# New durations in a list schedule, and a first attention head whose low parts are made on two engines

## The chip, the cores and the metric

The kernel runs on one core of one Trainium2 chip. The metric is the device time of one launch in microseconds (us), taken as the median of several runs. A core has five engines that run side by side, each through its own instruction queue, in order: TensorE (PE in the profile; PEld is its weight load), VectorE (DVE), ScalarE (ACT), GpSimd (POOL) and SyncE (SP, which here only issues DMA transfers). They wait for one another by semaphores.

## The reference

Three blocks follow each other. Attention of 2 batches x 8 heads over 768 positions with head size 64 is masked by a hash: a query sees only the keys whose six projection signs equal its own. Its output feeds two gated feed-forward blocks.

```python
q_bits = (np.einsum('bhsd,dk->bhsk', q, proj) > 0)     # 6 bits; k_bits likewise
mask = q_bucket[:, :, :, None] == k_bucket[:, :, None, :]
scores = np.where(mask, scale * q @ k.T, -1e9)
attn = softmax(scores) @ v                             # (1536, 512) over both batches
h = ((x @ w1) * (x @ w2)) @ w3 @ w_out                 # d_ff 1024
y = (sigmoid(h @ w_gate) * (h @ w_val)) @ w_out2       # d_ff 1536
```

The weights come as 64-bit floats and are decoded to 32 bits on the chip.

## The kernel before

**High and low parts.** TensorE multiplies in the 32-bit format fp32r in one pass. To keep the accuracy, an operand is split into a high part (a copy in fp32r) and a low part (the operand less its high part), and three products are added (`three`, L700): high x high, high x low, low x high. High parts are mostly ScalarE's work, low parts VectorE's or GpSimd's.

**Attention.** There are 16 heads of 6 blocks of 128 queries, 96 steps in all. For a step, `emit_qk` (L466) computes the scores of 128 queries by 768 keys in two banks of PSUM (L473, L476); the operands bq, bk, aq and ak hold the low parts, the keys and the hash rows, 64 partitions each, so that the mask is part of the products. `emit_max` (L478) takes the row maximum on VectorE (L482), `emit_exp` (L484) the exponential with the row sum on ScalarE (L492). `emit_T` (L517) transposes the result four tiles at a time on TensorE (L525), ScalarE copies them as high part (L528) and VectorE makes the low part (L530); both are called pt. `emit_av` (L534) multiplies them with v (L543). `emit_x` (L546) adds the two halves into xall with a small PSUM copy on ScalarE (256 elements, L555) and an addition on VectorE (L556).

**Heads.** `prep` (L399) readies a head one head ahead: GpSimd scales q (L409), copies (L410) and subtracts (L411); `hashes` (L388) multiplies with the projections (pq, L393), takes the sign on ScalarE (sg, L395) and compares patterns on TensorE (L396). The first head has nothing to hide behind and has its own code, `first_head` (L429): two loads of each half, ScalarE's high part (L448), VectorE's low part (L449), GpSimd's copies of k into bk and ak (L453), ScalarE's copy of bk's upper half (L454), the hashes, GpSimd's scaling into bq (L456), the thresholds on VectorE (L459) and ScalarE (L461). Its first activation (L437) makes ScalarE load its function table and writes to thr, a tile that holds two thresholds. The constants (L810 to L834) are emitted between its two parts; pq_raw holds the projections, loaded twice on ScalarE's DMA queue (L434, L435), and pq is made from it (L826, L827).

**Filler.** Beside attention, `gen_fill` (L563) decodes w3 and w_out and multiplies them into one matrix wc (wacc, L598), and `gen_first` (L626) runs the first of the three token groups of the first feed-forward block (p and y, through L703) once the first batch's attention is done. `decode` (L331) turns a 128x512 tile of 64-bit floats into 32 bits: two activations (L342, L343), two operations on GpSimd (L344, L345), a shift on VectorE (L346) and an addition (L351).

**The order.** The program is emitted with priorities (`prio`, L845: 100 per attention step). Then `order_engines` (L46) runs a list schedule over all instructions emitted so far: a small simulation in which every instruction has a duration by `cost` (L75), a step between engines (L97), the number of free buffers of each ring, and a DMA estimate (L222 to L225). Whenever an engine is free, it takes the ready instruction with the lowest priority number. The order that results is fixed on every engine, SP's DMA issues among them. It fixes the order alone, no times: on the chip an engine waits for the next instruction in its queue, whatever else is ready.

**The rest.** After the list schedule, `moe` (L718) emits the other token groups of the first block and the whole second block: 52 tiles of 36 matmuls of 512 columns (pa, pb and m, L703), with two, one or no decodes per tile.

Of the kernel before, what the change touches and what calls it, by code (L numbers as in the profile page):

```python
# [10 lines left out]
F32 = mybir.dt.float32  # L11
# [7 lines left out]
ALU = mybir.AluOpType  # L19
# [26 lines left out]
def order_engines(tc):  # L46
# [11 lines left out]
    def count(x):  # L58
        n = 1
        for _, c in list(x.ap)[1:]:  # L60
            n *= c
        return n
# [12 lines left out]
    def cost(k):  # L75
# [3 lines left out]
        banks = [x for x in rd + [i.outs[0]] if (region(x) or ("",))[0] in rings and rings[region(x)[0]][0][0] in ("psT", "psS")]  # L79
        if e == "PE":  # L80
            passes = 1 if "float32r" in str(rd[0].dtype) else 2 if n == 128 else 4
            return n / 2.4 * passes + (16 if passes == 1 else -12 if passes == 2 else 4)
        if e == "Activation":
            return 971 if n == 768 and banks else 50 + n * (0.836 if banks else 1.0)
        if e == "Pool":
            if op == "InstTensorTensor":
                return 40 + n * 2.4 if n < 768 else 2200
            return 100 + n * 1.15
        if e == "DVE":
            if op == "InstCustomDveAnt":  # L90
                return 720
            if op in ("InstTensorTensor", "InstTensorReduce") or (op == "InstTensorScalarPtr" and len(rd) > 1 and count(rd[1]) > 8):
                return 69 + n * (1.04 if banks else 1.4)
            return 585 if op == "InstTensorScalarPtr" and n == 384 else 69 + n * 0.6
# [141 lines left out]
def lsh_attention_moe_moe2_kernel(  # L236
# [47 lines left out]
    def f(ap):  # L284
        return ap.bitcast(F32)
# [12 lines left out]
    nthr = cst.tile([P, 1], F32, name="nthr")  # L298
    zb = cst.tile([P, 1], F32, name="zb")
# [129 lines left out]
    def first_head():  # L429
# [7 lines left out]
        act.activation(out=thr[:, 0:1], in_=zb, func=AF.Exp)  # L437
# [8 lines left out]
        for half in range(2):  # L446
            hs = slice(half * HS, (half + 1) * HS)
            act.activation(out=m["aq"][:, hs], in_=t[0][:, hs], func=AF.Copy, scale=scl[:, 0:1])  # L448
            dve.scalar_tensor_tensor(out=m["bq"][:, hs], in0=t[0][:, hs], scalar=scl[:, 0:1], in1=f(m["aq"][:, hs]),  # L449
                                     op0=ALU.mult, op1=ALU.subtract)  # L450
        load_qk(2)
        for d in ("bk", "ak"):
            pool.tensor_copy(m[d][0:D], t[1][0:D])  # L453
        act_copy(m["bk"][D:P], f(m["bq"][D:P]))  # L454
# [500 lines left out]
```

## Time and profile before

| | |
|---|---|
| median of 3 runs | 811.36 us (809.26 to 812.12) |
| the profiled execution's own time | 809.7 us |
| its span, first to last instruction | 807.5 us |
| granted TensorE clock in the profile | 1.00 of full speed |
| PE busy | 783.1 us (97%), 4016 matmuls |
| PEld busy | 657.3 us (81%) |
| DVE busy | 471.0 us (58%) |
| ACT busy | 512.4 us (63%) |
| POOL busy | 437.0 us (54%) |

A line of a table of groups gives the line of the kernel, the engine, the operation, the tile written and the tiles read, the shapes and the number of instructions; behind the first bar the busy time in us and the mean of one in ns; behind the second bar how long the engine sat idle just before these instructions, and what ended most of that. A timeline gives the start of a stretch of like instructions, how long it is, and how many there are (x2). A wait is named by who waited and who released it. Matmuls overlap, so a busy TensorE need not run at its densest.

### The profile page before, as it was taken

How to read it: one execution, taken by the hardware profiler on the slowest of the kernel's cores; microseconds unless marked ns; L12 is line 12 of the kernel's file. 1: busy time of each engine (PE TensorE's matmuls, PEld its weight loads, DVE VectorE, ACT ScalarE, POOL GpSimd, SP SyncE). 2: the span in 40 equal slices, each digit the busy share in tenths (PEclk: the TensorE clock that was granted, in tenths of full speed). 3: DMA queues.
4: the chain of work that ended last, by engine and by line, in shares of the span. 5: the costliest groups of instructions: out<-in, count | busy, mean ns of one | idle time of the engine just before them, and what ended most of it. 6: DMA issues, size and time to landing. Idle time of an engine off the chain costs nothing.

```text
span 807.5 us, 11531 instructions
## 1 busy us (share of the span) xinstructions
PE 783.1 (97%) x4016; PEld 657.3 (81%) x4016; DVE 471.0 (58%) x721; ACT 512.4 (63%) x946; POOL 437.0 (54%) x460
## 2 busy tenths in 40 slices
PE   5899999999999999999999999999999999999998
PEld 4787788888888888988888888888888888888886
DVE  5999997775989799773553535655422222222222
ACT  5999997785989888783465556767434333343332
POOL 6778885675576565286355556777523233332320
PEclk9999999999999999999999999999999999999999
DMA  8767676544456574130022123343001000010001
GB/s 263 200 180 184 170 209 170 141 110 109 108 148 167 131 178 118 39 113 0 27 79 78 53 79 105 124 137 105 0 1 53 0 1 1 0 53 1 0 1 52
DMA packets 28584, 74.44 MB, mean 92 GB/s; under 512 B 6128, under 2 KB 8432, under 8 KB 28528
## 3 DMA queue, kind: packets, MB, share of 16 engines
q1 hardware_dynamic: 28368, 73.73, 32.5%
q8 instruction: 31, 0.51, 0.3%
q14 instruction: 25, 0.20, 0.1%
q10 hardware_dynamic: 160, 0.00, 0.0%
HBM read 52.83 MB, written 3.19 MB: 69 GB/s over the span
## 4 chain that ended last, share of the span: by engine, by line
PE 82%; DVE 9%; ACT 3%; POOL 2%; issue 2%; DMA 0%; ACTq 0%; SPq 0%; DVEq 0%; POOLq 0%
PE m L703 18%; PE pa L703 18%; PE pb L703 18%; PE av L543 6%; PE tp L525 5%; PE p L703 5%; PE wacc L598 4%; PE y L703 3%; PE s L476 3%; PE s L473 3%; DVE pt L530 2%; DVE sm L482 2%; PE gps L393 1%; DVE w3f L351 1%; DVE da L346 1%
## 5 line engine op out<-in xcount | busy, mean ns | idle before, releaser
L743 DVE TENSOR_TENSOR pb<-pb,a 128x512 f32<-128x512 f32 x52 | 36.3, 699 | 178.0 <-PE pb L703 173.2
L697 POOL TENSOR_TENSOR wal<-xall,wah 128x512 fp32r<-128x512 f32 x36 | 47.6, 1323 | 107.0 <-ACT wah L282 107.0
L525 PE MATMUL tp<-idf,e 128*128 128x128 f32 x576 | 99.0, 274 | 2.8 <-DVE pt L530 1.5
L482 DVE TENSOR_REDUCE sm<-s 128x1 f32<-128x768 f32 x96 | 90.7, 947 | 17.6 <-PE s L476 17.4
L530 DVE TENSOR_TENSOR pt<-tp,pt 128x512 fp32r<-128x512 f32 x144 | 94.6, 680 | 9.5 <-ACT pt L528 8.7
L703 PE MATMUL pa<-x,wah 128*128 128x512 f32 x320 | 99.8, 391 | 0.0
L703 PE MATMUL pb<-x,wbh 128*128 128x512 f32 x320 | 98.6, 389 | 0.0
L492 ACT ACTIVATE e<-s,sm 128x768 f32<-128x768 f32 x96 | 86.8, 907 | 14.6 <-DVE sm L482 14.4
L344 POOL TENSOR_SCALAR dr<-st 128x512 bf16<-128x512 f32 x76 | 73.8, 981 | 40.8 <-issue 20.8
L528 ACT ACTIVATE pt<-tp 128x512 fp32r<-128x512 f32 x144 | 82.7, 601 | 10.7 <-PE tp L525 9.1
L525 PEld LDWEIGHTS tp<-idf,e 128*128 128x128 f32 x576 | 70.6, 140 | 13.9 <-DVE pt L530 4.3
L543 PE MATMUL av<-pt,spv 128*128 128x256 f32 x576 | 78.9, 286 | 2.8 <-DVE pt L530 2.6
L543 PEld LDWEIGHTS av<-pt,spv 128*128 128x128 f32 x576 | 73.0, 190 | 7.6 <-DVE pt L530 5.7
L703 PEld LDWEIGHTS pa<-x,wah 128*128 128x128 f32 x320 | 60.1, 188 | 13.6
L703 PEld LDWEIGHTS pb<-x,wbh 128*128 128x128 f32 x320 | 60.1, 188 | 12.6
L473 PE MATMUL s<-bk,bq 128*128 128x384 f32 x192 | 61.6, 370 | 4.6 <-ACT e L492 4.5
L598 PE MATMUL wacc<-wo,t 128*128 128x512 f32 x192 | 65.7, 414 | 0.2 <-POOL wo L593 0.2
L345 POOL TENSOR_SCALAR da<-da 128x512 f32<-128x512 f32 x76 | 48.8, 647 | 26.1 <-ACT da L342 22.5
L703 PE MATMUL pa<-x,wal 128*128 128x512 f32 x160 | 62.9, 393 | 0.0
L703 PE MATMUL pb<-x,wbl 128*128 128x512 f32 x160 | 62.3, 389 | 0.0
L476 PE MATMUL s<-ak,aq 128*128 128x384 f32 x192 | 60.3, 368 | 0.3 <-ACT aq L461 0.3
L343 ACT ACTIVATE dr<-st 128x512 int16<-128x512 uint32 x76 | 60.1, 790 | 0.0
(146 smaller groups left out, 1822.1 us busy)
## 6 DMA issues: line engine op xcount, KB each, us to landing
st<-in_moe_w_dram SPq DMA_DIRECT2D x32, 512.0 KB, 4.8
st<-in_moe_w_out_dram SPq DMA_DIRECT2D x20, 512.0 KB, 4.2
st<-in_moe_w_gate_dram SPq DMA_DIRECT2D x12, 512.0 KB, 3.3
st<-in_moe_w_val_dram SPq DMA_DIRECT2D x12, 512.0 KB, 3.2
qk<-in_qk_dram SPq DMA_DIRECT2D x15, 384.0 KB, 4.1
rawv<-in_v_dram SPq DMA_DIRECT2D x16, 192.0 KB, 2.5
rr<-row SPq DMA_DIRECT2D x16, 192.0 KB, 4.1
out_dram<-o SPq DMA_DIRECT2D x12, 256.0 KB, 2.0
```

Of the source, the lines that this page charges most:

```text
L343: act.activation(out=r.bitcast(I16)[:, 0::2], in_=lw, func=AF.Copy, scale=2.0 ** -29)
L344: pool.tensor_scalar(out=r.bitcast(BF16)[:, 1::2], in0=f(hw), scalar1=0.0, scalar2=1.0, op0=ALU.mult, op1=ALU.mult)
L473: pe.matmul(s[:, half, :HS], lhsT=m["bq"][:, qs], rhs=m["bk"][:, ks], start=True, stop=False)
L476: pe.matmul(s[:, half, :HS], lhsT=m["aq"][:, qs], rhs=m["ak"][:, ks], start=False, stop=True)
L482: dve.tensor_reduce(out=b, in_=s[:, :, :HS], op=ALU.max, axis=AX.XY, negate=True)
L492: act.activation(out=e.rearrange("p (a c) -> p a c", a=2), in_=s[:, :, :HS], func=AF.Exp, bias=sm, scale=1.0, accum_out=su_t[h][:, t:t + 1],)
L525: pe.transpose(ps[:, i * P:(i + 1) * P], e_t[g - g % 2 + a][:, c * P:(c + 1) * P], idf)
L528: act.activation(out=dh, in_=src, func=AF.Copy)
L530: dve.tensor_tensor(out=d, in0=src, in1=f(dh), op=ALU.subtract)
L543: pe.matmul(acc[:w.shape[1], :2 * P].rearrange("p (a t) -> p a t", a=2), lhsT=w, rhs=r[:, :, c], start=(c == 0 and i == 0), stop=(c == NT ...
L598: pe.matmul(acc, lhsT=t3[x][:, j], rhs=wo[y][:, j], start=(j == 0 and n == 0), stop=(j == NF1 - 1 and n == 2))
L703: mm = pe.matmul(ps, lhsT=lhs[x], rhs=rhs[y], start=start and n == 0, stop=stop and n == 2)
```

## The change

The durations in `cost` are replaced for several kinds of instruction: among them the exponential's 971 ns becomes 890, a small PSUM copy of 256 elements on ScalarE goes from 264 to 415, the six operations of a decode and GpSimd's work get other values, and TensorE's fixed parts change by a few ns. The first activation writes to a tile of its own (warm) and no longer to thr. In `first_head`, half 0 is split as before; of half 1, GpSimd scales q in place, ScalarE copies the high part without a scale, and GpSimd subtracts. ScalarE now copies k into bk's lower half, VectorE copies bk's upper half, and GpSimd copies k into ak. Nothing else is edited; the order of the instructions is computed anew from the new durations.

```diff
--- before.py
+++ after.py
@@ -77,21 +77,30 @@
         rd = [x for x in i.ins if hasattr(x, "ap")]
         n = max([count(i.outs[0])] + [count(x) for x in rd[:1]])
         banks = [x for x in rd + [i.outs[0]] if (region(x) or ("",))[0] in rings and rings[region(x)[0]][0][0] in ("psT", "psS")]
+        es = mybir.dt.size(i.outs[0].dtype)
         if e == "PE":
             passes = 1 if "float32r" in str(rd[0].dtype) else 2 if n == 128 else 4
-            return n / 2.4 * passes + (16 if passes == 1 else -12 if passes == 2 else 4)
+            return n / 2.4 * passes + (18 if passes == 1 else -20 if passes == 2 else 4)
         if e == "Activation":
-            return 971 if n == 768 and banks else 50 + n * (0.836 if banks else 1.0)
+            if banks:
+                return 890 if n == 768 else 490 if n == 512 else 300 + n * 0.45
+            return 70 + n + (100 if es == 2 else 0)
         if e == "Pool":
             if op == "InstTensorTensor":
-                return 40 + n * 2.4 if n < 768 else 2200
-            return 100 + n * 1.15
+                return 100 + n * 2.45 if n < 768 else 2250
+            if op == "InstTensorCopy":
+                return 640 if n == 384 else 100 + n * 0.9
+            return 340 if n < 64 else 110 + n * 1.15 + (190 if es == 2 else 0)
         if e == "DVE":
             if op == "InstCustomDveAnt":
-                return 720
-            if op in ("InstTensorTensor", "InstTensorReduce") or (op == "InstTensorScalarPtr" and len(rd) > 1 and count(rd[1]) > 8):
-                return 69 + n * (1.04 if banks else 1.4)
-            return 585 if op == "InstTensorScalarPtr" and n == 384 else 69 + n * 0.6
+                return 860
+            if op == "InstTensorReduce":
+                return 69 + n * 1.06
+            if op == "InstTensorTensor" or (op == "InstTensorScalarPtr" and len(rd) > 1 and count(rd[1]) > 8):
+                return 150 + n * 0.9 if banks else 100 + n * 1.45
+            if op == "InstTensorScalarPtr" and n == 512 and "int32" in str(i.outs[0].dtype):
+                return 560
+            return 595 if op == "InstTensorScalarPtr" and n == 384 else max(125, 69 + n * 0.6)
         return 600
 
     step = {("Activation", "DVE"): 145, ("Activation", "PE"): 200, ("Activation", "Pool"): 170, ("DVE", "Activation"): 132,
@@ -296,6 +305,7 @@
     thr = cst.tile([P, 2], F32, name="thr")
     scl = cst.tile([P, 1], F32, name="scl")
     nthr = cst.tile([P, 1], F32, name="nthr")
+    warm = cst.tile([P, 1], F32, name="warm")
     zb = cst.tile([P, 1], F32, name="zb")
     pat = cst.tile([P, P], F32R, name="pat")
 
@@ -434,7 +444,7 @@
         act.dma_start(out=pq_raw[0:D], in_=proj)
         act.dma_start(out=pq_raw[D:P], in_=proj)
         dve.memset(zb, -2.0 ** -64)
-        act.activation(out=thr[:, 0:1], in_=zb, func=AF.Exp)
+        act.activation(out=warm, in_=zb, func=AF.Exp)
         for half in range(2):
             hs = slice(half * HS, (half + 1) * HS)
             sync.dma_start(out=t[0][:, hs], in_=qk[0][:, hs])
@@ -443,15 +453,17 @@
         load_qk(1)
         load_v(0)
         yield
-        for half in range(2):
-            hs = slice(half * HS, (half + 1) * HS)
-            act.activation(out=m["aq"][:, hs], in_=t[0][:, hs], func=AF.Copy, scale=scl[:, 0:1])
-            dve.scalar_tensor_tensor(out=m["bq"][:, hs], in0=t[0][:, hs], scalar=scl[:, 0:1], in1=f(m["aq"][:, hs]),
-                                     op0=ALU.mult, op1=ALU.subtract)
+        h0, h1 = slice(0, HS), slice(HS, S)
+        pool.tensor_scalar(out=t[0][0:D, h1], in0=t[0][0:D, h1], scalar1=0.0, scalar2=SCALE, op0=ALU.add, op1=ALU.mult)
+        act.activation(out=m["aq"][:, h0], in_=t[0][:, h0], func=AF.Copy, scale=scl[:, 0:1])
+        dve.scalar_tensor_tensor(out=m["bq"][:, h0], in0=t[0][:, h0], scalar=scl[:, 0:1], in1=f(m["aq"][:, h0]),
+                                 op0=ALU.mult, op1=ALU.subtract)
+        act_copy(m["aq"][:, h1], t[0][:, h1])
+        pool.tensor_tensor(out=m["bq"][:, h1], in0=t[0][:, h1], in1=f(m["aq"][:, h1]), op=ALU.subtract)
         load_qk(2)
-        for d in ("bk", "ak"):
-            pool.tensor_copy(m[d][0:D], t[1][0:D])
-        act_copy(m["bk"][D:P], f(m["bq"][D:P]))
+        act_copy(m["bk"][0:D], t[1][0:D])
+        dve.tensor_copy(m["bk"][D:P], f(m["bq"][D:P]))
+        pool.tensor_copy(m["ak"][0:D], t[1][0:D])
         pss = [hashes(m, half) for half in range(2)]
         pool.tensor_scalar(out=m["bq"][D:P], in0=t[1][D:P], scalar1=0.0, scalar2=SCALE, op0=ALU.add, op1=ALU.mult)
         for half in range(2):
```

## Rows read from the trace of the kernel before

**Rows 1.** Busy us (instructions) of PE, PEld, DVE, ACT, POOL by stretch; clock, DMA share, GB/s

```profile
20.00:100.00 80.00, 74.15 (x482) 63.83 (x483) 77.12 (x119) 75.42 (x151) 64.63 (x77) 1.00 0.72 186
100.00:200.00 100.00, 96.54 (x581) 83.88 (x580) 76.57 (x113) 77.90 (x151) 66.35 (x80) 1.00 0.56 147
200.00:300.00 100.00, 97.06 (x623) 86.35 (x622) 88.80 (x136) 88.92 (x177) 62.35 (x78) 1.00 0.59 147
...
345.00:800.00 455.00, 454.98 (x1986) 371.89 (x1985) 178.77 (x265) 222.38 (x376) 213.35 (x185) 1.00 0.13 45
```

**Rows 2.** TensorE's waits in 20 to 345 us: total us, times, longest

```profile
PE s L473 <- ACT e L492: 3.4, 6, 1.4
PE av L543 <- DVE pt L530: 2.6, 5, 0.8
PE gps L393 <- DVE pt L530: 1.8, 2, 1.3
PE tp L525 <- DVE pt L530: 1.5, 3, 0.7
```

**Rows 3.** Timeline of the start: start us, us, engine, line, operation

```profile
3.51 0.06 DVE L828 MEMSET thr<- 64x1 f32 x1 [2.20 <-ACT thr L437]
...
4.10 1.12 ACT L448 ACTIVATE aq<-qk,scl 128x384 fp32r<-128x384 f32 x2 [0.65 <-DVE scl L834]
...
5.47 0.17 DVE L826 CAST pq<-pq_raw 64x6 fp32r<-64x6 f32 x1
...
5.79 0.98 PE L393 MATMUL gps<-aq,pq 128*128 128x384 f32 x2 [5.79 <-DVE pq L826]
5.82 0.82 POOL L453 CAST bk<-qk 64x768 fp32r<-64x768 f32 x1 [3.85 <-DMA qk<-in_qk_dram]
5.87 2.27 DVE L449 SCALAR_TENSOR_TENSOR bq<-qk,scl,aq 128x384 fp32r<-128x384 f32 x2
6.59 1.15 POOL L453 CAST ak<-qk 64x768 fp32r<-64x768 f32 x1
...
7.59 0.52 PE L393 MATMUL gps<-aq,pq 128*128 128x384 f32 x1
8.18 0.84 ACT L282 ACTIVATE bk<-bq 64x768 fp32r<-64x768 f32 x1 [2.95 <-DVE bq L449]
...
9.04 1.05 ACT L395 ACTIVATE sg<-gps,zb 128x384 fp32r<-128x384 f32 x2
9.11 0.84 POOL L456 TENSOR_SCALAR bq<-qk 64x768 fp32r<-64x768 f32 x1 [1.37 <-ACT bk L282]
...
11.11 1.16 ACT L461 ACTIVATE aq<-gps,nthr 64x384 fp32r<-64x384 f32 x2 [1.02 <-DVE ak L459]
```

**Rows 4.** Line view of L435, the second load into pq_raw

```profile
L435 ACTq DMA_DIRECT2D pq_raw<-in_proj_dram x1: 611/611/611, 1.3 to 1.3; - x1
...
DMA to landing us min/median/max: 4.1/4.1/4.1
```

**Rows 5.** Groups by line and form in 20 to 100 us, of ACT, DVE, POOL

```profile
L492 ACT ACTIVATE e<-s,sm 128x768 f32<-128x768 f32 x26 | 23.5, 905 | 2.6 <-DVE sm L482 2.5
L343 ACT ACTIVATE dr<-st 128x512 int16<-128x512 uint32 x12 | 9.6, 796 | 0.0
...
L282 ACT ACTIVATE xall<-av 64x256 f32<-64x256 f32 x13 | 5.0, 381 | 0.3
...
L351 DVE CUSTOM_DVE_ANT_0 wor<-da,dr 128x1024 uint16<-128x1024 uint16 x8 | 6.3, 790 | 0.0
...
L411 POOL TENSOR_TENSOR bq<-qk,aq 128x384 fp32r<-128x384 f32 x10 | 10.1, 1014 | 0.8
L344 POOL TENSOR_SCALAR dr<-st 128x512 bf16<-128x512 f32 x11 | 9.4, 853 | 0.6
```

**Rows 6.** Timeline of TensorE near 41 us

```profile
40.70 0.27 PE L525 MATMUL tp<-idf,e 128*128 128x128 f32 x1
...
40.99 0.71 PE L525 MATMUL tp<-idf,e 128*128 128x128 f32 x5
```

## The prediction, made before the change was run

> **What bounds the kernel now.** I read the busy table by stretches first, because the change can only act where its instructions run. From 345 us on TensorE is busy 454.98 of 455 us [rows 1]: the two MoE stages are fed without a gap, they are emitted after the list schedule, and no edit touches them. What can move lies ahead of that. In 20 to 100 us TensorE is busy 74.15 of 80 us while VectorE and ScalarE are busy 77.12 and 75.42: there the two elementwise engines are the limit. In 100 to 200 and 200 to 300 us TensorE is busy 96.54 and 97.06 of 100, with VectorE at 77 and 89: TensorE bounds, and loses time only where its queue comes to a matmul whose operand is late. Idle TensorE time in these three stretches is 5.85 + 3.46 + 2.94 = 12.25 us. This is what a better order can win in gaps that show; a busy TensorE can also run below its densest spacing, so it is no strict bound.
>
> Then I asked what ended those gaps [rows 2]. VectorE's low part of the transposed probabilities (pt, L530) ended 2.6 + 1.8 + 1.5 = 5.9 us of them, the exponential (e, L492) 3.4 us. So the gaps come from elementwise results that the order puts later than TensorE's queue assumes. Last I read the first 12 us as a timeline [rows 3], for the first head.
>
> **Part 1, the warm-up activation gets its own tile.** Before, the Exp that loads the table wrote thr, so VectorE's memset of thr waited for it 2.20 us, with all the constants, scl and the pq copies queued behind [rows 3]. That wait goes. What is late next is the second small load into pq_raw: issued at 1.3 us and landing 4.1 us later, at 5.4 [rows 4]. Its copy at 5.47 is what the first matmul at 5.79 needs (pq is one tile), and in the planner's arithmetic the pq copies are due before the first low part, so in VectorE's queue that low part still stands behind them, at 5.87 [rows 3]. The 2.20 us are therefore worth 0 here; if that load landed early, they would be worth up to 2.20 us at the first low part, which I do not expect, as the issue is not touched.
>
> **Part 2, low parts on two engines.** Before, both low parts of bq are VectorE's: two of 2.27 / 2 = 1.14 us, so they end at about 7.0 and 8.14 [rows 3]. ScalarE's copy of bk's upper half stands ahead of the Sign in its queue, waits for the second low part, and runs 8.18 to 9.02. So the Sign starts only at 9.04, although the hash matmuls of half 0 end at 7.59 + 0.52 = 8.11 [rows 3]. After: the copy that waits for bq is VectorE's, and ScalarE copies the half of bk that needs only the loaded k (there at 5.82, since GpSimd starts on it then; 0.84 us, so it ends near 6.7). Sign of half 0 can then start at about 8.11 + 0.2 = 8.3, 0.74 us sooner. The 0.2 is my allowance for the step from TensorE to ScalarE; VectorE's end at 8.14 to ScalarE's start at 8.18 bounds such a step below, by 0.04.
>
> Half 1: GpSimd now scales 64x384 (half of the elements of the bk cast that took 0.82 us, so some 0.4 to 0.6), ScalarE makes aq (both halves were loaded by 4.66, the start of its second at the latest), and GpSimd makes the low part. The planner has the ak copy due before aq of half 1, so GpSimd does the copy first: 5.82 + 0.82, or 1.15 when it is disturbed, then one subtraction of 128x384 at 1014 ns [rows 5]: it ends between 7.7 and 8.0. That leaves half 1 no later than the 8.14 of before. Sign of half 1 follows half 0's, each half of the 1.05 us pair, and ends at 9.4 to 9.75 instead of 10.09. Behind it the chain is the same code, up to the ReLU at 11.11 [rows 3]. GpSimd's scaling of bq at 9.11 now waits for VectorE's copy, which no row of 64x768 prices; between 0.35 (nothing but the shorter half of ScalarE's 0.84) and 1.15 (the slowest of the same shape) I take 0.84, the same shape on ScalarE. It starts at 8.0 and ends at 8.9, so 9.11 holds. **I take 0.7 us gained**, between 0 and 1.5. It persists, because the stage behind it is bound by VectorE and ScalarE, which then start sooner.
>
> What speaks against this part is a row: each VectorE low part took 1.14 us while GpSimd's two casts ran beside it, and GpSimd's second cast of the same shape took 1.15 us beside it against 0.82 for the first [rows 3]. The first low part ends 0.4 us after the first cast does. So the two engines seem to take turns, and "at the same time" may not be had. [...] Taking turns in full, cast 0.82, low part 0.4, subtraction 1.01 from 5.82 give 8.05 for half 1, still not after 8.14; hence the 0.7 stands, and comes from ScalarE's queue more than from the second engine.
>
> **Part 3, new durations in the planner.** The instructions of the rest stay; their order on each engine, the SP queue's DMA issues among them, is computed anew. A decode cost the planner 562 + 562 (ScalarE), 689 + 689 (GpSimd) and 376 + 720 (VectorE) = 3598 ns and now costs 582 + 682, 889 + 699 and 560 + 860 = 4272 (the new 560 for int32 also applies to uint32, as it is asked for by name). The trace has means of 796 for the int16 one, 853 for the bf16 one, 790 for the addition into wor [rows 5]. The small PSUM copy goes from 264 to 415, the trace's mean being 381. In 20 to 100 us there are about 12 decodes: VectorE is now planned 12 x 324 = 3.9 us longer in 80 us, GpSimd 12 x 210 = 2.5, ScalarE 12 x 140 = 1.7 plus 13 copies x 0.151 = 2.0 and less 26 exponentials x 0.081 = 2.1 (971 to 890). So in the old plan VectorE had some 5% of room that the chip did not have [rows 1], and the planner pulled fill work of later steps into it, ahead of the low parts for which TensorE then waited. With the room gone, less is pulled ahead.
>
> The price: between all of the 12.25 us of gaps won and as much lost (nothing in the trace excludes a worse order). The gaps that this error makes are the 5.9 us behind pt. Half of these is my value, **3.0 us**, nearer to the small end, because the exponential's 3.4 us, TensorE's own order and the loads are not what was repriced. What is late next is the exponential behind the row maximum, on the same two engines.
>
> **Sum.** 0 + 0.7 + 3.0 = 3.7 us. The profiled execution took 809.7 us, with a span of 807.5; it would become 806.0 and 803.8. The median of the three runs is 811.36, 1.7 above the profiled one, and loses the same: **807.7 us**. About 0.3%, 2.4 us, is what a measurement of this kernel can tell from no change.
>
> **Rivals.**
> - *The new order only moves gaps* (0.27): the first head gives its 0.7 or nothing, and waits won in one stretch return in another, since 20 to 100 us has no room on VectorE in any order. 810.7 us. For it: the stage after 345 us needs the same work whatever the order. Against it: gaps of 2.94 to 5.85 us in stretches with the same kinds of work say that order matters.
> - *Slower, by transposes priced too short* (0.20). Five transposes in a row took 0.71 us with a last one of 0.27, so 0.11 us each [rows 6]. The planner had 94.7 ns and now has 86.7: its TensorE is now further ahead of the chip's, while VectorE and ScalarE are priced right. It would plan the attention products right behind low parts that are in truth ready, or late, by other amounts, and place its fill matmuls where no gap is. The added error is 8 ns x 576 transposes = 4.6 us; if each of it became waiting, with the first head's 0.7, the time is 811.4 + 4.6 - 0.7 = 815.3. It decides if TensorE's waits for pt grow in 100 to 300 us, where it bounds. Against it: TensorE waits in order, so a transpose that takes longer than planned also gives pt more time.
> - *The first head gains nothing* because the two engines take turns longer than above or ScalarE's queue places bk's copy between the two Signs (half 1 then at about 10.1 as before): 808.4 with the reorder's gain, 811.4 without. A chance of 0.08 stands for it beside the reorder's gain; beside no gain it is part of the first rival.
> - *A larger gain*: all gaps behind pt go and the first head's 0.7: 811.4 - 5.9 - 0.7 = 804.8; it is part of the forecast's chance.
>
> **Numbers.** Forecast with the larger gain: 0.45, of which 0.03 falls within 0.3%. First head nothing: 0.08, faster. Only moved: 0.27, all within. Slower: 0.20, of which 0.18 goes beyond 0.3%, the rest within. That gives faster 0.50, same 0.32, slower 0.18. The range runs from 802.0 (the 5.9 us behind pt, half of the exponential's 3.4 and 1.5 at the start: 811.4 - 5.9 - 1.7 - 1.5 = 802.3) to 815.0 (just short of the slow rival in full). The forecast's own range is 803 to 809.5.
>
> **What would show it.** Right: Sign of the first head at 8.3 instead of 9.04, no wait of VectorE for thr, the first matmul still near 5.8; TensorE's idle time in 20 to 300 us near 9 us, with the waits for pt halved; TensorE full from 345 us or a little before, and the MoE stages as long as now. Wrong: a first matmul much before 5.5 (then the pq load was not the gate); Sign at 9.0 or later; idle time in 100 to 300 us above 8 us with more waits for pt (the slow rival); or a TensorE full from the same 345 us although the gaps moved.

## The result and the profile after

Six runs of the changed kernel have a median of 820.06 us (819.39 to 824.5), six of the kernel before, on the same chip, 811.0. The ratio is 1.0121, interval [1.0107, 1.0135]: slower by 1.2%, where a gain of 0.5% was forecast; it lies outside the range. The profiled execution took 819.47 us, with a span of 817.6 against 807.5 us. So 10.1 us are to be explained.

The busy table by stretches, to be held against [rows 1]: stretch, its length, then busy us (instructions) of PE, PEld, DVE, ACT, POOL, the granted clock, the DMA share, GB/s.

```profile
20.00:100.00 80.00, 70.18 (x450) 61.52 (x448) 74.74 (x112) 69.75 (x138) 54.46 (x68) 0.96 0.66 176
100.00:200.00 100.00, 95.18 (x582) 83.79 (x583) 79.67 (x117) 82.23 (x160) 67.77 (x82) 1.00 0.55 144
200.00:300.00 100.00, 97.29 (x622) 86.96 (x621) 85.03 (x131) 85.50 (x170) 62.45 (x74) 1.00 0.56 142
345.00:800.00 455.00, 452.35 (x1978) 368.13 (x1977) 184.02 (x270) 225.10 (x381) 215.58 (x189) 1.00 0.14 47
```

In 20 to 100 us TensorE does 450 matmuls where it did 482, VectorE and ScalarE are less busy too, and the granted clock is below 1.00 for the first time. In 200 to 300 us nothing is lost. From 345 us on, 2.65 us are idle where 0.02 was. TensorE's waits in 20 to 345 us (total us, times, longest), to be held against [rows 2]:

```profile
PE s L485 <- ACT e L504: 7.1, 5, 2.6
PE wacc L610 <- ACT wo L291: 1.9, 1, 1.9
PE tp L537 <- DVE ft L428: 1.3, 2, 0.7
PE wacc L610 <- ACT t L291: 1.2, 1, 1.2
PE av L555 <- DVE ft L428: 1.0, 1, 1.0
PE av L555 <- DVE pt L542: 0.9, 2, 0.5
PE wacc L610 <- POOL wo L605: 0.9, 1, 0.9
...
PE gps L403 <- DVE pt L542: 0.3, 1, 0.3
PE tp L537 <- DVE pt L542: 0.2, 1, 0.2
```

The waits for pt fell from 5.9 to 1.4 us. What took their place are waits for the exponential, 7.1 where it was 3.4, for decoded weights (wo, t), 4.0 where it was 0.2, and for the hash rows of a coming head (ft), 2.3 where it was 0.5.

The start of the changed kernel as a timeline (start us, us, engine, line, operation, and in brackets the idle time before and who ended it), to be held against [rows 3]:

```profile
5.40 0.17 DVE L838 CAST pq<-pq_raw 64x6 fp32r<-64x6 f32 x1 [1.64 <-DMA pq_raw<-in_proj_dram]
...
5.66 0.82 POOL L466 CAST ak<-qk 64x768 fp32r<-64x768 f32 x1 [1.29 <-DMA qk<-in_qk_dram]
...
5.72 0.66 PE L403 MATMUL gps<-aq,pq 128*128 128x384 f32 x1 [5.72 <-DVE pq L838]
5.80 2.05 DVE L459 SCALAR_TENSOR_TENSOR bq<-qk,scl,aq 128x384 fp32r<-128x384 f32 x1
6.45 0.99 POOL L462 TENSOR_TENSOR bq<-qk,aq 128x384 fp32r<-128x384 f32 x1
...
8.96 0.58 ACT L405 ACTIVATE sg<-gps,zb 128x384 fp32r<-128x384 f32 x1 [2.48 <-PE gps L403]
...
11.63 0.58 ACT L405 ACTIVATE sg<-gps,zb 128x384 fp32r<-128x384 f32 x1
...
15.73 0.90 ACT L504 ACTIVATE e<-s,sm 128x768 f32<-128x768 f32 x1
```

VectorE's wait for thr is gone and its pq copy waits for the load instead, so the first matmul stays at 5.72. The low part of half 0 now takes 2.05 us where each took 1.14, and ends at 7.85, 0.41 us after GpSimd's subtraction does (6.45 + 0.99 = 7.44). The second Sign starts at 11.63, and the first exponential at 15.73; before it was at 14.1.

**Where the 10.1 us arise.** I took the same instruction (the k-th exponential, attention product, or product of the later stage) in both traces and subtracted the starts. The change is behind by 1.6 us at the first exponential, by 8.6 at the product that stood at 146.2 us before, by 5.2 at 353 us, by 8.6 at 421.6 us and by 10.1 at 795. So: 1.6 us at the start, 7.0 lost between there and some 150 us (most of it by 105), 3.4 won back up to 353 us, 3.4 lost between 353 and 421 us, 1.5 after that. Their sum is 10.1. This sets one execution against one other; two executions of the same order can differ by some us at such a point, as a pair of runs below shows.

### The profile page after: what moved, and what is told of

It is laid out like the page before. It is cut to its first block, busy times and chain, and to the rows that moved or that the text cites. A ratio compares the mean times of both kernels' runs of the same rounds, so it can differ in the third digit from the quotient of the medians.

```text
span 817.6 us, 11540 instructions
## 1 busy us (share of the span) xinstructions
PE 783.8 (96%) x4016; PEld 660.1 (81%) x4016; DVE 476.7 (58%) x721; ACT 515.0 (63%) x946; POOL 435.1 (53%) x461
## 4 chain that ended last, share of the span: by engine, by line
PE 82%; DVE 8%; ACT 4%; issue 2%; DMA 2%; POOL 1%; SPq 0%; ACTq 0%; DVEq 0%; POOLq 0%
PE m L715 18%; PE pb L715 17%; PE pa L715 17%; PE av L555 6%; PE tp L537 5%; PE p L715 5%; PE wacc L610 3%; PE s L485 3%; PE s L488 3%; PE y L715 2%; DVE pt L542 2%; PE gps L403 2%; DVE sm L494 1%; DMA rr<-row 1%; ACT pt L540 1%
```

## The experiments

What was weighed: that the new durations give a worse order (by transposes priced too short, or otherwise); that the first head's new code costs, at the start or by what it does later; and that any new plan moves the time by some us either way. An expectation calls them theories A, B and C. It also names earlier runs by short labels, which stand in brackets where these runs are told. Medians and ratios are against the kernel before, on the same chip, with 95% intervals. "Behind by" is always the difference of starts against the kernel before, as above. Where medians of two runs are subtracted, they can come from different chips; the kernel before had medians of 810.7 to 811.9 us on them, so such a difference is good to about 1 us. In the cuts of code, `...` stands for lines left out.

**The parts.** Only `cost` changed, with the old head and no warm tile (e1):

> The new durations on the first head of before. Theory A (the new durations give a worse order): most of the 9 us loss is here, 816 to 819 us, with TensorE idle some 4 us more in 20 to 100 us and a gap of 2 to 3 us near 365 us at the start of the MoE part. Theory B (the first head's later start, 1.6 us, and the order that follows from it): 811 us or less, within 2 us of before. Theory C (any new order lands a few us away, up or down): between 805 and 819, not the same losses in the same places as in the changed kernel.

812.25 us, ratio 1.0019 [1.0004, 1.0035]. Only the head and the warm tile changed, with the old durations:

> The new first head with the durations of before. Theory A: 812 to 813 us, the 1.6 us of the later first exponential and no more, the gaps after 20 us as in before. Theory B: 816 to 820. Theory C: the start is 1 to 2 us late and the rest lands anywhere between 806 and 818. In all of them the second half's subtraction on GpSimd and the first half's on VectorE take turns: the VectorE one ends after 7.4 us as in the changed kernel, if GpSimd's order is the same.

819.25 us, 1.0102 [1.0085, 1.0118]. Of these two the head is the one that loses, although its code ends before 15 us: in this run the first exponential is 0.8 us early, and the kernel is still 7.2 us behind from 127 us on. (The turns that the expectation names did not happen here: VectorE's low part began at 5.12 us, ahead of GpSimd's copy at 5.43, and took 0.62 us.) The new durations alone are 2.7 us ahead at 353 us in their trace (a gain of the size forecast) and 2.0 behind at 421 us. Where the head-only kernel loses, near 60 us, as a timeline:

```profile
60.29 2.70 POOL L518 TENSOR_TENSOR xall<-xall,rr 128x768 f32<-128x768 f32 x1 [3.23 <-DMA rr<-row]
...
62.94 0.50 POOL L411 CAST aq<-qk 128x384 fp32r<-128x384 f32 x1
...
63.49 0.69 PE L394 MATMUL gps<-aq,pq 128*128 128x384 f32 x1 [2.60 <-POOL aq L411]
```

and its busy table from 63.1 us on (columns as in the table of stretches above; the number behind POOL's is the clock):

```profile
63.10:69.90 6.80, 6.33 (x20) 5.64 (x21) 1.64 (x3) 3.08 (x7) 5.00 (x7) 0.50 0.55 125
```

GpSimd normalises two finished heads (xall by rr, `emit_scale`) and waits 3.23 us for the load of rr, which landed 9.3 us after its issue (6.3 in the kernel before, which has no wait there). Behind it in GpSimd's queue stands the readying of a coming head (aq), and TensorE's queue has come to that head's hash product. TensorE stalls 2.60 us, and then has a granted clock of 0.50, the half clock below, for 6.8 us. That is most of the loss: 0.6 us behind at 58.6, 5.8 at 77.7.

**Is it any new plan?** One step time of the planner, 10 ns more, in the old kernel:

```diff
-("PE", "Activation"): 197
+("PE", "Activation"): 207
```

> The kernel of before with one planner figure changed by 10 ns (the step from TensorE to ScalarE, 197 to 207), which says nothing truer or falser of the chip. Theory A: 810 to 812 us, as before. Theory C: the order changes in many places and the time moves by 2 us or more, either way (805 to 817).

812.77 us, 1.0015 [1.0, 1.003]. Only TensorE's new fixed parts (the transposes' price among them):

```diff
-return n / 2.4 * passes + (16 if passes == 1 else -12 if passes == 2 else 4)
+return n / 2.4 * passes + (18 if passes == 1 else -20 if passes == 2 else 4)
```

> Only TensorE's new durations (transposes 8 ns shorter, one-pass matmuls 2 ns longer), all else as before. The prediction's slow rival (transposes priced too short, TensorE's waits for pt grow in 100 to 300 us) expects up to 815 us. Theory A without that rival: 810 to 812. Theory C: a move of 2 us or more either way.

812.69 us, 1.0023 [1.0009, 1.0037]. These two new plans cost 0.2% each, not 1.2%. The transposes' price costs no more than that, alone or with all the other new durations (the first run, 1.0019). The slow rival as I had priced it is out.

**The warm tile, and its address.** Old kernel with the warm tile alone:

```diff
+warm = cst.tile([P, 1], F32, name="warm")
...
-act.activation(out=thr[:, 0:1], in_=zb, func=AF.Exp)
+act.activation(out=warm, in_=zb, func=AF.Exp)
```

> The kernel of before with the tile warm alone (no other edit of the first head, old durations). The tile takes 32 bytes of each partition and moves all tiles behind it, xall and wc among them, by 32 bytes. Address theory, from the runs of the changed kernel and of the new head alone, where the matmuls of 430 to 600 us stood 2 to 5 ns further apart than before: the same spacing here (100 us of 500 to 600 hold 432 matmuls instead of 436), 1.5 to 2 us lost behind 400 us, 812.5 to 813.5 us. Rival (the slower spacing comes from the order of the decodes' work, not from addresses): spacing as before, 811 to 812 us. The wait of VectorE for thr is gone in both, and the first matmul is not earlier than the second load into pq_raw.

813.26 us, 1.0024 [1.0008, 1.004]. It is 0.5 us ahead at 380 us and 1.3 behind at 611, with the instructions of that stretch in the same order: it loses 1.8 us where nothing waits. The tile stands among the constants and so, as I reckon, moves all tiles allocated behind them; no run prints addresses, so neither that nor by how much is shown. So I let the Exp write to a third column of thr, with no tile more, first in the head-only kernel:

```diff
-thr = cst.tile([P, 2], F32, name="thr")
+thr = cst.tile([P, 3], F32, name="thr")
...
-warm = cst.tile([P, 1], F32, name="warm")
...
-act.activation(out=warm, in_=zb, func=AF.Exp)
+act.activation(out=thr[:, 2:3], in_=zb, func=AF.Exp)
```

> The new first head with the old durations, the Exp writing to a third column of thr, so that no address moves. Address theory: the 1.7 us behind 400 us come back, and the loss ahead of 100 us stays (the normalisation of the first heads on GpSimd waiting for its row load near 60 us, TensorE idle behind it and then at half clock): 817 to 818 us. Rival: 819 as with the tile.

816.72 us, 1.0053 [1.0031, 1.0074], from nine executions between 812.5 and 818.7 and one of 1103.68, which the ratio leaves out. Its first exponential is 1.5 us late where that of the head-only kernel was 0.8 early, with the same order on VectorE, GpSimd and the DMA issues. When the loads land decides: VectorE's second copy from pq_raw ran at 5.61 us instead of 4.72, so the low part of half 0 began at 6.01, behind GpSimd's copy (5.86), and took 2.04 us instead of 0.62. The same edit in the changed kernel:

> The changed kernel with the Exp writing to a third column of thr, so that all addresses are those of before. By the runs so far the spacing of 500 to 600 us returns to 435 or 436 matmuls, and 1.5 to 1.8 us come back: 818 to 818.7 us.

818.53 us, 1.0096 [1.0076, 1.0117]. The busy rows of 500 to 600 us, first of the warm tile alone, then of the changed kernel with the third column:

```profile
500.00:600.00 100.00, 100.00 (x430) 80.50 (x429) 50.90 (x80) 60.09 (x101) 61.67 (x61) 1.00 0.24 78
```

```profile
500.00:600.00 100.00, 100.00 (x436) 81.51 (x435) 53.64 (x85) 62.84 (x106) 65.43 (x65) 1.00 0.27 89
```

TensorE is busy without a gap in both and starts 430 or 436 matmuls (435 in the kernel before). Each of the six profiled kernels with the extra tile falls back by 1.6 us between 421 and 611 us, and each of the thirteen without it by 0.0. That the tile costs this is shown: 1.5 us of the 10.1 in the changed kernel. That it does so by the addresses it moves is my inference, since the instructions of that stretch and their order are the same; no run shows an address, or why one would matter there.

**The first head's pieces.** Only the low part of half 1 (and its scaling) to GpSimd, in the old kernel:

```diff
...
+pool.tensor_scalar(out=t[0][0:D, h1], in0=t[0][0:D, h1], scalar1=0.0, scalar2=SCALE, op0=ALU.add, op1=ALU.mult)
...
+act_copy(m["aq"][:, h1], t[0][:, h1])
+pool.tensor_tensor(out=m["bq"][:, h1], in0=t[0][:, h1], in1=f(m["aq"][:, h1]), op=ALU.subtract)
```

> Old durations, old copies of k into bk and ak, old thr; only the low part of half 1 goes to GpSimd, with its scaling. If the split is the harmful part: GpSimd's three operations and VectorE's low part take turns, the first Sign is at 9 us or later, and the kernel is 815 to 820. If it is not: 810 to 813.

818.75 us, 1.008 [1.0052, 1.0108]. Its start as a timeline:

```profile
5.53 0.82 POOL L455 CAST bk<-qk 64x768 fp32r<-64x768 f32 x1 [1.16 <-DMA qk<-in_qk_dram]
5.59 1.75 DVE L828 CAST pq<-pq_raw 64x6 fp32r<-64x6 f32 x1
6.32 0.99 POOL L452 TENSOR_TENSOR bq<-qk,aq 128x384 fp32r<-128x384 f32 x1
...
7.48 0.66 PE L393 MATMUL gps<-aq,pq 128*128 128x384 f32 x1 [7.48 <-DVE pq L828]
```

VectorE's copy of 64x6 elements, 0.17 us before, takes 1.75: it starts with GpSimd's cast and ends with GpSimd's subtraction. VectorE did not get in between the two GpSimd instructions. In the kernel before, where GpSimd had two copies instead of a copy and a subtraction, it did: there the first low part ended at about 7.0 us, during GpSimd's second copy, which took 1.15 us instead of 0.82 (6.59 to 7.74). The first matmul comes 1.7 us later, the first exponential 3.4, and the half clock follows in 30.0 to 33.4 us.

Only the copies moved, in the old kernel (e8), and the same with the Exp in the third column:

```diff
-for d in ("bk", "ak"):
-    pool.tensor_copy(m[d][0:D], t[1][0:D])
-act_copy(m["bk"][D:P], f(m["bq"][D:P]))
+act_copy(m["bk"][0:D], t[1][0:D])
+dve.tensor_copy(m["bk"][D:P], f(m["bq"][D:P]))
+pool.tensor_copy(m["ak"][0:D], t[1][0:D])
```

> Old durations, both low parts on VectorE as before, old thr; only the copies move (bk lower half to ScalarE, bk upper half to VectorE). By the prediction's account of ScalarE's queue this gives the Sign at about 8.3 instead of 9.04 us and 0.7 us at the start: 810 to 811 us if the order behind it stays good. If any shift of the first head by a microsecond changes which load the normalisation near 60 us waits for, it may be 814 to 819 as well.

> Old durations, moved copies, third column of thr. The first exponential 1 us or so sooner than before (13.1 to 13.6). If nothing behind it stalls: 809.5 to 810.5 us, faster than both kernels; by e8 (812.0, the same without the third column) rather 811 to 813.

812.02 us, 1.001 [0.9992, 1.0028], and 811.79 us, 1.0007 [0.999, 1.0024]. The first exponential is 0.9 and 1.5 us early, the third 1.1 and 0.4 late. So a gain at the first head is real and is gone two steps later. Where it goes, the third step shows, as a timeline of this kernel (third column) and then of the kernel before:

```profile
13.63 0.69 PE L473 MATMUL s<-bk,bq 128*128 128x384 f32 x1 [1.11 <-ACT e L492]
...
14.97 0.84 PE L393 MATMUL gps<-aq,pq 128*128 128x384 f32 x2
...
17.95 0.96 DVE L482 TENSOR_REDUCE sm<-s 128x1 f32<-128x768 f32 x1 [4.43 <-PE s L476]
```

```profile
15.14 0.45 PE L473 MATMUL s<-bk,bq 128*128 128x384 f32 x1 [1.18 <-ACT e L492]
...
15.88 0.51 PE L393 MATMUL gps<-aq,pq 128*128 128x384 f32 x2
...
17.59 0.96 DVE L482 TENSOR_REDUCE sm<-s 128x1 f32<-128x768 f32 x1 [2.64 <-PE s L476]
```

From the step's first score product to its row maximum the same products, in the same order on TensorE, take 17.95 - 13.63 = 4.32 us here and 17.59 - 15.14 = 2.45 before: 1.9 us more, as much as the gain that is lost between the first and the third exponential. TensorE is the limit there: it is busy without a gap (5.80 of 5.80 us in 13.8 to 19.6). A pair of matmuls of 384 columns takes 0.84 us here, as at a granted clock of 0.50 (the head-only kernel has such a pair at 66.02 us, in its half-clock stretch), and 0.51 before. The first stretch with the full clock, 1.00, begins in the trace's clock records at 19.65 us here and at 13.75 in the kernel before; in 10 to 13.7 us TensorE was busy 2.49 us here and 3.43 there. It is not this trace alone: in the thirteen traces with an edited first head the full clock begins at 15.5 to 23.2 us, in those with the old one at 13.0 to 13.8 (five) or at 18.2 and 18.6 (two). Why it begins later, no run shows.

The changed kernel with both low parts on VectorE again (e9):

```diff
...
-pool.tensor_tensor(out=m["bq"][:, h1], in0=t[0][:, h1], in1=f(m["aq"][:, h1]), op=ALU.subtract)
+for half in range(2):
+    hs = slice(half * HS, (half + 1) * HS)
+    act.activation(out=m["aq"][:, hs], in_=t[0][:, hs], func=AF.Copy, scale=scl[:, 0:1])
+    dve.scalar_tensor_tensor(out=m["bq"][:, hs], in0=t[0][:, hs], scalar=scl[:, 0:1], in1=f(m["aq"][:, hs]),
+                             op0=ALU.mult, op1=ALU.subtract)
```

> The changed kernel with one part undone: both low parts of the first head are VectorE's again; new durations, the moved copies and the warm tile stay. If the split is what costs (the run with it alone gave 818.75, the run with the copies alone 812.0): 811 to 815 us, with the 1.7 us of the moved addresses in it, and the first exponential at 13 to 14 us. If the loss belongs to the whole of the new order: 818 to 821.

817.43 us, 1.0081 [1.0061, 1.0101]: the first exponential is 1.5 us early, and the kernel 8.3 behind at 97.3 us. Then the changed kernel with one edit that keeps GpSimd free beside VectorE's low part:

```diff
-pool.tensor_copy(m["ak"][0:D], t[1][0:D])
+act_copy(m["ak"][0:D], t[1][0:D])
```

> The changed kernel with the copy of k into ak on ScalarE instead of GpSimd, so that GpSimd has nothing between its scaling and its low part. Turn-taking theory: GpSimd's subtraction runs from about 5 to 6 us, VectorE's low part ends by 6.6 us instead of 7.85, the first Sign stands near 8 us instead of 8.96 and the first exponential 1 us or more sooner than 15.73; the whole kernel 1 to 4 us below 820, if the order behind stays alike. Rival (VectorE's low part is slow by itself, or for its operand): it ends at 7.5 or later again.

816.13 us, 1.0075 [1.0051, 1.01]. Its start as a timeline:

```profile
5.04 0.99 POOL L462 TENSOR_TENSOR bq<-qk,aq 128x384 fp32r<-128x384 f32 x1 [0.64 <-ACT aq L291]
...
6.29 0.62 DVE L459 SCALAR_TENSOR_TENSOR bq<-qk,scl,aq 128x384 fp32r<-128x384 f32 x1
...
8.01 0.58 ACT L405 ACTIVATE sg<-gps,zb 128x384 fp32r<-128x384 f32 x1 [0.86 <-PE gps L403]
...
13.39 0.90 ACT L504 ACTIVATE e<-s,sm 128x768 f32<-128x768 f32 x1 [1.01 <-DVE sm L494]
```

With GpSimd idle beside it the low part takes 0.62 us instead of 2.05, and the Sign starts at 8.01. So the turns are shown, and the first exponential comes 15.73 - 13.39 = 2.3 us sooner without them. The whole gains 3.9 us by it (820.06 - 816.13), and 5 us are still lost, with the head now early: they are lost behind it.

**The wait behind the load of rr.** The planner lets an instruction be held behind another. I held GpSimd's normalisation of a pair of heads behind the readying of the first head of the pair after the next, first in the head-only kernel (e11) and then in the kernel before:

```diff
...
+for p in range(NH // 2 - 2):
+    Tiles.holds.append((late["scale", p].name, late["bq", 2 * p + 4].name))
 order_engines(tc)
```

> The new first head with the old durations (819.25 us), and the planner held back so that GpSimd's normalisation of a pair of heads stands behind the readying of the head two further on, not ahead of it. If the loss near 60 us is GpSimd's queue (it waited 3.2 us for the row load, and TensorE 2.6 us for the readying behind it, and then ran at half clock): no such wait, no half clock near 63 us, 812 to 815 us. If the loss comes with the later loads whatever stands in GpSimd's queue: 817 to 820.

817.93 us, 1.0092 [1.0072, 1.0113]. The wait near 60 us and the half clock are gone (0.8 us behind at 77.7, where the head-only kernel had 5.8), but it is 4.5 behind at 97.3, 3.0 at 237.6 and 5.8 at 299.1. So this wait was where that trace lost its time, but the order that comes without the wait loses nearly as much elsewhere.

> The kernel of before with the hold alone. If the hold only changes the place of an operation that nobody is waiting for: 810 to 812. If it costs by itself (the 3 us that e11 lost behind 230 us): 813 to 815.

812.7 us, 1.0009 [1.0, 1.0019]. In the old order, where the load was in time, the hold is worth nothing.

**Put together.** New durations, old head, third column:

> New durations, first head of before, and the Exp in a third column of thr (no wait of VectorE for it, no moved address). If the planner's new figures are worth what the trace of e1 showed ahead of 345 us (2.5 us) and lose it again at the handover to the MoE part (VectorE and GpSimd taking turns there, a half clock of 3.4 us): 810 to 813 us. If the start a little sooner lets another stall happen ahead of 105 us: 814 to 818.

813.01 us, 1.0000 [0.9989, 1.0011]. In its trace it is 4.9 us behind at 105 us and 1.5 behind at 353, although VectorE, ScalarE, GpSimd and the DMA issues have the very order of the first run, which was 2.7 ahead there. So one order can come out 4 us apart in two executions, and the 2.7 us are not a gain to count on. New durations, moved copies, third column, the hold, and both low parts on VectorE (e14):

> New durations, moved copies, both low parts on VectorE, third column of thr, and GpSimd's normalisation held behind the readying of the head two further on. If the stall near 67 us of e9 (TensorE waiting 2.6 us for that readying) is the normalisation ahead of it: the stall is gone and the kernel is 809 to 813. If not: 815 to 817 as e9 without its 1.7 us of addresses.

805.71 us, 0.9914 [0.9897, 0.993]: faster than both. The same without the hold, and the same with the low parts split (which is the changed kernel with the third column and the hold):

> e14 without the hold. If the hold is what let the new durations keep their gain: TensorE stalls again between 60 and 105 us behind GpSimd's readying, and the kernel is 812 to 817 us (e9, the same with moved addresses, was 817.4, of which 1.7 are addresses: 815.7). If the hold did little and e14 was fast for its copies and durations: 805 to 808.

> e14 with the second low part on GpSimd, that is, the changed kernel with the hold and the third column. If the split costs by the start it delays (first exponential 1.5 us later than before against 0.7 earlier in e14) and by what follows from it: 808 to 814, 2 to 8 us over e14. If the split costs nothing once the stall is gone: 805 to 807.

817.01 us, 1.0064 [1.0044, 1.0083], and 810.57 us, 0.9981 [0.9969, 0.9992]. So with the new durations the hold is worth 817.01 - 805.71 = 11.3 us, and the split costs 810.57 - 805.71 = 4.9. The timeline of the kernel without the hold, where it loses:

```profile
63.61 2.23 POOL L524 TENSOR_TENSOR xall<-xall,rr 128x768 f32<-128x768 f32 x1 [3.13 <-DMA rr<-row]
...
66.84 0.45 PE L402 MATMUL gps<-bq,pq 128*128 128x384 f32 x1 [2.42 <-POOL bq L420]
...
100.59 0.44 PE L482 MATMUL s<-bk,bq 128*128 128x384 f32 x1 [2.91 <-ACT e L501]
...
101.47 2.50 POOL L524 TENSOR_TENSOR xall<-xall,rr 128x768 f32<-128x768 f32 x1 [2.29 <-DMA rr<-row]
```

and its busy table behind these two stalls (the clock is the number behind POOL's):

```profile
67.80:71.20 3.40, 3.40 (x16) 3.30 (x14) 1.68 (x4) 2.34 (x5) 3.16 (x5) 0.51 0.85 173
101.90:105.30 3.40, 3.40 (x14) 2.95 (x14) 2.13 (x3) 2.82 (x7) 3.40 (x3) 0.50 0.14 54
```

The first stall is the chain of the head-only kernel again: the load of rr late, GpSimd standing, the coming head's bq behind it, a stall of TensorE, the half clock. The second is another: TensorE waits 2.91 us for an exponential, and the late load of rr comes only behind that. With the hold the order on GpSimd is the other way round (timeline of the kernel with the hold):

```profile
62.94 1.02 POOL L420 TENSOR_TENSOR bq<-qk,aq 128x384 fp32r<-128x384 f32 x1
64.68 2.26 POOL L524 TENSOR_TENSOR xall<-xall,rr 128x768 f32<-128x768 f32 x1 [0.72 <-DVE sm L491]
...
101.08 1.02 POOL L420 TENSOR_TENSOR bq<-qk,aq 128x384 fp32r<-128x384 f32 x1
102.06 2.22 POOL L524 TENSOR_TENSOR xall<-xall,rr 128x768 f32<-128x768 f32 x1
```

Neither normalisation waits for its load, and neither half-clock stretch is there (one of 3.4 us at 24.5 is left). At 353 us this kernel is 4.1 us ahead of the one before, and the kernel without the hold 2.7 behind. The two have the same order up to the first of these normalisations and differ on every engine behind it, so the 11.3 us are what the whole new order is worth: of the 9.8 us by which the traces part between 58.6 and 421.6 us, 4.5 arise by 77.7, with the first stall.

Lined up so that each kernel differs from the one ahead of it by one edit, the runs give the change in steps (third column of thr up to the last step): new durations 1.0000, with the moved copies 1.0064, with the low parts split 1.0096, with the tile warm 1.0121, each known to about 0.2%. The moved copies alone are 1.0007. So half of the loss comes from two edits that cost nothing one by one, and the hold turns just that pair into a gain (0.9914).

## Why the prediction was wrong

**Part 1** was right about what is late next and wrong in its price. The load of pq_raw gates the first matmul, as predicted, at 5.72. But "worth 0" left out what a tile of its own does later: it costs 1.6 us in the stages that "no edit touches".

**Part 2** failed in the step that Sign of half 0 "can then start at about 8.11 + 0.2 = 8.3", and in "it persists". The first took over from the kernel before that VectorE's low part of half 0 ends at about 7.0. Half 1's own low part was not late: GpSimd ended it at 7.44, ahead of the 8.14 of before. I had the warning row, 1.14 us for a low part beside GpSimd's casts, and took turns in full for GpSimd's work alone: cast 0.82, low part 0.4, subtraction 1.01. On the chip VectorE got no turn between GpSimd's two instructions; the low part of half 0 ended last, at 7.85 instead of 7.0, and Sign started at 8.96 instead of 8.3. The second Sign, forecast to end at 9.4 to 9.75, only started at 11.63, because the ReLU of half 0 (11.03 us) stands ahead of it in ScalarE's queue, and the pattern product of half 0 (9.59) ahead of half 1's last two hash products (10.08) in TensorE's: the code behind the first Sign is the same, its order is not. A low part that took 0.62 us with GpSimd idle beside it (e10) took 2.05 here, over GpSimd's copy and the subtraction behind it. The rival that had the engines take turns longer gave this too little weight: in it the first head merely gained nothing, at 808.4 or 811.4 us. "It persists" is refuted by the moved copies alone, whose 1.5 us were gone at the third exponential. Its reason was that the stage behind is bound by VectorE and ScalarE; in that stretch VectorE waits 4.43 us for scores, and TensorE, with 0.84 us for a pair of matmuls that took 0.51 before, is the limit. The prediction had no term for when its full clock begins (19.65 us there, 13.75 before).

**Part 3** was right in its mechanism as far as the waits go: those for pt fell from 5.9 to 1.4 us, more than the half I took, and with the new durations alone one trace was 2.7 us ahead at 353 us, against the 3.0 of the sum (the other, of the same order, was 1.5 behind). What failed is the 3.0 us itself, "half of these": it counted the waits that go and nothing for what is late next. TensorE's idle time in 20 to 300 us was to fall from 12.25 to about 9 us and rose to 17.35. I named the exponential; it went from 3.4 to 7.1 us. I did not look at the end of the list schedule, the handover to the stage behind it. TensorE's waits of the changed kernel in 345 to 400 us:

```profile
PE pa L715 <- DVE x L698: 1.8, 1, 1.8
PE pa L715 <- POOL wal L709: 0.8, 1, 0.8
```

VectorE makes the last low parts of x there (up to 1.79 us each) while GpSimd makes those of the weights (1.70 to 1.74), and TensorE arrives before they are done. The new durations alone lose 4.7 us between 353 and 421 us, with the half clock at 358.0 to 361.4 among it; the changed kernel 3.4; the best kernel 1.1.

**What the sum had no term for** is the price of one stall in 20 to 105 us. There VectorE and ScalarE are busy over 9 us in 10, as [rows 1] showed, so there is little room to catch up, and a stall of TensorE can be followed by the half clock. In the changed kernel TensorE works 2.83 of 5 us in 20 to 25 and 2.27 of 5 in 75 to 80, and then:

```profile
25.70:29.10 3.40, 3.40 (x17) 3.24 (x16) 3.00 (x5) 2.56 (x5) 2.60 (x4) 0.50 0.23 70
80.30:83.70 3.40, 3.38 (x13) 2.92 (x13) 1.82 (x4) 2.29 (x5) 3.32 (x4) 0.50 0.48 141
```

By my estimate from the granted clock of 0.50, 3.4 us do the work of 1.7 there, so these two cost up to 3.4 us beside the stalls themselves (12 products with v take 2.78 us at 26.64, and 1.59 at 70.48, where the clock is 1.00). Not every such stretch is followed by the half clock: TensorE works 2.50 of 5 us in 360 to 365, and the clock is 1.00 in 365 to 370. The stall before 80 us is in part a decode that comes late: a shift on VectorE that took 0.52 us at 70.8 took 1.54 beside GpSimd's subtraction (timeline of the changed kernel), so wor and then wo are late, and the product that was to fill TensorE waits. The 1.0 us more explain about half of its wait of 1.87:

```profile
73.80 1.30 POOL L605 TENSOR_TENSOR wo<-wor,wo 128x512 fp32r<-128x512 f32 x1 [1.66 <-ACT wo L291]
...
73.84 1.54 DVE L356 TENSOR_SCALAR da<-da 128x512 uint32<-128x512 uint32 x1
...
77.39 0.63 ACT L291 ACTIVATE wo<-wor 128x512 fp32r<-128x512 f32 x1 [0.96 <-DVE wor L361]
...
78.08 0.50 PE L610 MATMUL wacc<-wo,t 128*128 128x512 f32 x1 [1.87 <-ACT wo L291]
```

The new `cost` has a duration for each operation, but none of them has the turns of two engines (a low part of 2.05 us beside GpSimd, 0.62 without). The planner cannot see this, nor a load that is later than its estimate, nor TensorE's clock.

**The rivals.** The slow one was right in its sign, short in its size (815.3) and wrong in its mechanism: the waits for pt did not grow, and TensorE's prices alone cost 0.2%. "Only moved" describes the new durations alone (1.0000 with the Exp in the third column). My test "idle time in 100 to 300 us above 8 us" was not met either (4.82 + 2.71 = 7.5). I looked for the loss where TensorE bounds; it arose in 20 to 105 us, where the other engines do.

**What stays open.** That the rr chain costs the kernel without the hold its time near 67 us is seen in its trace; how much of the 11.3 us is this chain and how much the rest of the new order, no run separates, and in the head-only kernel taking the chain away gave back 1.3 us (819.25 to 817.93). In the changed kernel itself that wait is 0.4 us only. The hold takes 818.53 - 810.57 = 8.0 us off it as well (third column in both; the ratios differ by 1.15%, 9.3 us), and the stall for wo is gone with it. So of the changed kernel's loss the tile and the split are shown as parts, and the half that comes with the durations and the moved copies together lies in the order, as the hold shows; at which wait it arises is not shown. Why the third-column head kernel spreads over 6 us was not settled either; that its start depends on when one load lands may be a part of it.

## What to carry to other kernels

A list schedule with truer durations is only as good as what it leaves out: engines that take turns (2.05 us for a low part of 0.62), loads that land late (9.3 us after the issue instead of 6.3), a full clock that begins late (19.65 us instead of 13.75). Look first at where an in-order engine waits for a load with the bottleneck's work queued behind it, and put that work ahead; here one such rule was worth 11 us together with the new durations and the moved copies, and each of the three alone was worth nothing (1.0009, 1.0000, 1.0007). Before work is split over VectorE and GpSimd "at the same time", look at what else GpSimd has next to it; and give a scratch value a free column of an existing tile rather than a new tile, which cost 1.6 us here. A gain at the start of a kernel can be lost to a full TensorE clock that begins later: compare the time that the same products behind it take.

## What was not expected of the hardware

- VectorE stood for two GpSimd instructions in a row, a copy and a subtraction: a copy of 64x6 took 1.75 us (0.17 alone), a low part of 128x384 2.05 (0.62).
- TensorE's full clock began at 19.65 us instead of 13.75 in a kernel whose first exponential was 1.5 us sooner.
- With one more small tile among the constants, TensorE started 430 or 431 matmuls of 512 columns in 100 us instead of 435 or 436, with no wait and at full clock.
- TensorE's granted clock was 0.50 for 3.4 us after it had worked 2.27 of 5 us (75 to 80 us of the changed kernel), and for 6.8 us after a wait of 2.60 us (the head-only kernel). No such stretch is in the profile before between 20 and 800 us.
- Loads of rr, all alike, landed between 3.1 and 10.2 us after their issue within one execution (the kernel without the hold).
